# A gMLP kernel whose first column block is written out in one order, with a fourth raw tile and earlier loads

## The chip, the cores and the metric

The kernel runs on one core of one Trainium2 chip, in one launch. The metric is the device time of that core in microseconds. TensorE (PE) multiplies matrices out of SBUF into PSUM banks (8 of 128 x 512 fp32 here), VectorE (DVE) and ScalarE (ACT) work elementwise, GpSimd (POOL) and SyncE (SP) issue DMAs, and ACT issues some too. Each engine takes its instructions in the order in which the program holds them; an instruction that waits holds what stands behind it on its engine.

## The reference

The layer has two halves, each with an adaptive layer norm: a state space convolution (half A), whose code the change leaves alone, and a gated MLP (half B) over 2048 tokens of width 576 with 4608 hidden columns. Half B is what this text is about:

```python
z = _gelu(jnp.einsum("bsd,df->bsf", x, w_in))
z1 = z[..., :Fh]
z2 = _layernorm(z[..., Fh:], axis=-1)
g = jnp.einsum("ts,bsf->btf", w_sp, z2) + b_sp[None, :, None]
return jnp.einsum("bsf,fd->bsd", z1 * g, w_out)
```

`Fh` is 2304, `w_sp` is 2048 x 2048 and mixes tokens, so g needs the whole of z2 before its first column can be made.

## The kernel before, in words

Half A and the making of z2 fill the first 692 us. z2 lies then in memory (`z2_d`), normalized. What follows, `phase_b` (line 1629), takes the output tokens in four **column blocks** q = 0 to 3 of 512. All products are made in fp16 with a high and a low part: a fp32 matrix X becomes hi = fp16(X) and lo = X - hi, and a product takes three matmuls (hi hi, hi lo, lo hi). For w_sp x z2 and for w_in x the input, a scheme of seven products in place of eight is used, so each operand is first turned into seven tiles of sums: this is a **set** (`zset`, 128 x 7 x 2 x 256 fp16).

In one block, nine steps f = 0 to 8 each do the following.
- Two **z1 units**: gelu(x w_in) for 128 columns each. In block 0 this is `z1_unit`: 14 matmuls 128 x 512 with weights `wf` loaded from `win_d`. In blocks 1 to 3 it is `z1_pair` with a set of w_in (`zset` again, 42 matmuls with `n2o`), plus 6 matmuls `ps<-n2r,wr` for the last 64 rows of w_in; those rows (`wr`) are loaded by SP (`wr_load`) and scaled on ACT (`wr_scale`, L1427). PE's results are copied by ACT (L1461), summed by DVE (L1458) and put through gelu on ACT.
- **g_products**: g = w_sp x z2 for 256 columns, four **groups** n = 4f to 4f + 3 of 42 matmuls 128 x 256, `ps<-wsp,zset`, 168 in all, into four PSUM banks. Each group has its own set of z2; the eight tiles `wsp` of w_sp belong to the block.
- **g_unit**, the gate: DVE adds the products with the bias into the single tile `gt` (six instructions, L1525), multiplies with z1 (L1540), ACT writes the high part (L1542), DVE subtracts (L1544), ACT writes the low part (L1546). The next step's products need the banks that L1525 frees.

After the nine steps `out_block` multiplies with w_out (`ps<-wout,z`, 432 matmuls 128 x 288), while DVE and ACT build the next block's `n2o` and `wsp` tiles; each half row of output passes ACT (L1574) and DVE (L1575 to L1577) and a whole row is written by a DMA that ACT issues (L1604).

**Where the sets come from.** In block 0 each set of z2 is built: SP loads 512 KB into a tile `raw` (`z2_load`), DVE forms the sums (L1036, L1037), ACT the high part (L1091), DVE the low part (L1092), which frees the raw tile. Two sets of three are then stored to `set_d` by a DMA that ACT issues; groups with n % 3 == 2 are built again in block 1 and stored there. All others are loaded by POOL (L1489). In block 1 the sets of w_in are built too: four DMAs into a raw tile (`wa_raw`), DVE L1411 to L1414, ACT L795, DVE L801. The raw tiles also take the reads of `w_spT`, from which the next block's `wsp` tiles are made, and other transfers: three tiles in all. A load that has no free tile waits on SP's queue, with every load behind it.

**What sets the order.** The products on PE are pinned in the order of the program (line 129 is the helper that pins, so pinned instructions carry L129). In block 0, `ahead` is called for each group: it asks for the set three further on (`ready`), whose load is issued `AHEAD` = 3 built sets ahead (`more`). The rest on DVE and ACT is placed by a scheduler of the framework, from the instructions that could go next. In `out_block` and its builds DVE, ACT and PE are all pinned (`self.nc = self.last`).

Of the kernel before, what the change touches and what calls it, by code (L numbers as in the profile page):

```python
# [765 lines left out]
class Mlp:  # L766
# [270 lines left out]
        V.tensor_tensor(r[:, 5:7], r[:, 1:4:2], r[:, 4:5].to_broadcast([128, 2, 256]), op=ALU.subtract)  # L1037
# [44 lines left out]
    def z2_load(self, n):  # L1082
        self.nc.sync.dma_start(self.raw(("a", n))[:, :4].rearrange("p k n -> p (k n)"), self.z2_d[n // 4, n % 4].rearrange("p s g c -> p s (g c)"))

    def z2_build(self, n):

        nc = self.nc
        r = self.wss.pop(("a", n))
        o = self.bp.tile([128, 7, 2, 256], F16, name="zset", bufs=3)
        self.z_sums(r)  # L1090
        nc.scalar.activation(o[:, :, 0], r, AF.Copy)  # L1091
        nc.vector.tensor_tensor(o[:, :, 1], r, o[:, :, 0], op=ALU.subtract)  # L1092
        return o


    def x1_load(self, b):
# [320 lines left out]

    def wr_load(self, f):

        wr = self.wrs[f] = self.fp.tile([128, 2, 2, 128], F16, name="wr", bufs=2)  # L1420
        self.nc.sync.dma_start(wr.rearrange("p h k c -> p h (k c)"), self.win_d[f:f + 10:9, :, 8:10].rearrange("h p k c -> p h (k c)"))

    def wr_scale(self, f):

        for h in range(2):
            w, b = self.wrs[f][:, h], R_C + (f + 9 * h) // 4
            self.nc.scalar.activation(w, w, AF.Copy, scale=self.col(b))  # L1427
# [67 lines left out]
    def g_products(self, q, f):  # L1495
# [3 lines left out]
        for i in range(8):  # L1499
            if i % 2 == 0:  # L1500
                n = 4 * f + i // 2
                z = self.zset.pop((q, n))
                if q == self.kept_in(n):
                    self.nc.scalar.dma_start(self.set_d[f, i // 2], z)
                self.ahead(q, n)
# [9 lines left out]
    def g_unit(self, q, f, pg, parts=1):  # L1515
# [11 lines left out]
        def both(pm):  # L1527
            return pm.rearrange("p (o n) -> p o n", o=1).to_broadcast([128, 2, 256])

        add(g1, both(p17[:, 0]), self.bsp[q], neg)  # L1530
        add(g2, both(p6[:, 0]), g1)
        add(g1[:, 0], p54[:, 0], g2[:, 0])
        add(g1, p32, g1)
        add(g2, both(p17[:, 1]), g2, neg)
        add(g2, p54, g2)
# [3 lines left out]
        for c in cs:  # L1539
            V.scalar_tensor_tensor(gt[:, :, c], gt[:, :, c], self.qcol(q, S_P), z1[:, :, c], op0=ALU.mult, op1=ALU.mult)  # L1540
        for c in cs:
            A.activation(p[:, :, 0, c], gt[:, :, c], AF.Copy)  # L1542
        for c in cs:
            V.tensor_tensor(gt[:, :, c], gt[:, :, c], p[:, :, 0, c], op=ALU.subtract)  # L1544
        for c in cs:
            A.activation(p[:, :, 1, c], gt[:, :, c], AF.Copy, scale=2048.0)  # L1546

    def wout_load(self, f):

# [1 line left out]
        self.wss["out", f] = t  # L1551
        self.nc.sync.dma_start(t, self.I["w_out"][128 * f:128 * f + 128])

    def wout_split(self, f):
        self.split(self.wout[:, f, 0], self.wout[:, f, 1], self.wss.pop(("out", f)), self.col(S_O), act=True)

    def out_products(self, pm, q, tt, h, fs):
        T = self.nc.tensor
# [23 lines left out]
    def out_block(self, q):  # L1582
# [5 lines left out]
        for n, (tt, h) in enumerate(halves):  # L1588
# [5 lines left out]
            for k in range(3) if n == 2 else () if n < 2 else (n,):  # L1594
# [8 lines left out]
                elif h == 1:  # L1603
                    A.dma_start(self.out[b], xt)  # L1604

    def phase_b(self):
        self.nc = self.most = Mixed(self.tc, self.tied, "tensor")
        self.last = Mixed(self.tc, self.tied, "vector", "scalar", "tensor")
# [36 lines left out]
        def ahead(q, n):  # L1645
# [1 line left out]
            if isinstance(n, tuple):  # L1647
                return
            f, i = divmod(n, 4)
            if i == 0 and f < 8 and q == 0:  # L1650
                for k in range(units(q, f), units(q, f + 1)):
                    if (q, order[k]) not in self.wfs:
                        self.z1_load(q, order[k])
            if q == 0:
                if ("out", n - 6) in self.wss:
                    self.wout_split(n - 6)
                if 4 <= n < 22:
                    self.wout_load(n - 4)
# [5 lines left out]
        self.ahead = ahead  # L1664
        order = [f + 9 * k for f in range(9) for k in range(2)]

        def units(q, f):

            return max(6, 2 * f + 2)
# [6 lines left out]
        self.wsp_read(self.raw(("b", 7))[:, :4], 0, 7)  # L1676
        more(0, 2)
        self.wsp_build(0, 7)
        for i in range(3, 6):
            self.z1_load(0, order[i])  # L1680
        ready(0, 2)
        for q in range(4):
            done = 0

            def z1(n):
                nonlocal done
                while done < min(n, 18):
                    self.z1_unit(q, order[done])
                    done += 1

            for f in range(9):
# [3 lines left out]
                if q == 0:  # L1695
                    z1(units(q, f))
                else:
                    self.z1_pair(q, f)
                if f == 8 and q < 3:
                    if q == 0:  # L1700
                        self.cfp.close()
                        self.fp = self.pool(self.ctx, "fq", 1, side="right")
                pg = self.g_products(q, f)
                if q and f < 8:
                    self.wr_scale(f + 1)
                if f < 8:
                    self.g_unit(q, f, pg)
                if q == 0:
                    if f == 5:
                        for i in (6, 7):  # L1710
                            self.wsp_load(1, i, None)
                            self.norm_sp(1, i)
                elif q < 3 and f < 6:
# [11 lines left out]
            for i in range(8):  # L1725
                if i == 1:
                    self.scale_gate(q)
                    self.g_unit(q, 8, pg, 2)
                if q < 3:
                    if i == 1:  # L1730
                        self.n2_build(q + 1, 1)
                    self.wsp_build(q + 1, i)
                    block(q + 1, i + 3 if i > 1 else i + 2)
                    if i == 1:
                        self.rows_load(q, 1)
                        block(q + 1, 4)
# [76 lines left out]
```

## Time and profile before

| | us |
|---|---|
| median of 3 runs (1894.89 to 1903.77) | 1895.33 |
| the profiled execution | 1892.11 |
| its span, first to last instruction | 1890.2 |
| PE busy in it | 1702.1 |
| DVE busy | 1268.3 |
| ACT busy | 842.0 |

The mean granted clock of TensorE is 0.961 of full. Times in the views are us from the span's start. A row of a timeline has start, duration, engine, line, operation, output and inputs, the number of instructions run together, and in brackets the idle time before with what ended it. A row of the grouped lines has busy time and mean ns of one, and behind the second bar the idle time before, by releaser. A row of the waits has who waited on what: total, times, longest.

### The profile page before, as it was taken

The numbers are of one execution on the slowest core, as the hardware profiler recorded it, in microseconds if no ns is written. First come the engines' busy times: TensorE is split into PE (matmuls) and PEld (weight loads), VectorE is DVE, ScalarE is ACT, GpSimd is POOL, SyncE is SP. The second block draws the span as 40 slices with busy tenths as digits, with TensorE's granted clock in tenths as the row PEclk, the third lists the DMA queues.
The fourth block names the chain that finished last, engine by engine and source line by source line (L and its number), as shares of the span: only waits on it lengthen the run. The fifth ranks groups of instructions, "written<-read, shape, count | busy, mean of one in ns | idle before, by whom it ended". The sixth has DMA issues, their size and how long they took to land. (4 is left out here: it accounts for less than half of the span.)

```text
span 1890.2 us, 35620 instructions
## 1 busy us (share of the span) xinstructions
PE 1702.1 (90%) x14766; PEld 1257.7 (67%) x14766; DVE 1268.3 (67%) x2352; ACT 842.0 (45%) x1078; POOL 236.8 (13%) x376
## 2 busy tenths in 40 slices
PE   2597999996999998888997968789999999999998
PEld 1254555564555446666676857678888888888887
DVE  8886999848999975866577564657644457544432
ACT  3678999834776663443333323233322213311110
POOL 3211222332222110000000000000011110011100
PEclk9788999998999999998998989999999999999999
DMA  9466556697797885755554656566566564555531
GB/s 251 149 198 204 150 141 166 181 267 239 235 295 250 235 246 191 258 186 189 194 167 155 242 186 219 193 223 208 186 233 221 205 216 154 171 199 207 204 124 39
DMA packets 186914, 377.02 MB, mean 199 GB/s; under 512 B 37536, under 2 KB 107424, under 8 KB 185984
## 3 DMA queue, kind: packets, MB, share of 16 engines
q1 hardware_dynamic: 141840, 157.31, 27.9%
q0 software_dynamic: 36128, 171.57, 27.3%
q10 hardware_dynamic: 8784, 45.86, 6.2%
q8 instruction: 116, 1.90, 0.4%
q14 instruction: 46, 0.38, 0.1%
HBM read 263.94 MB, written 101.31 MB: 193 GB/s over the span
## 5 line engine op out<-in xcount | busy, mean ns | idle before, releaser
L129 PEld LDWEIGHTS <-zset 128*128 128x128 f16 x7182 | 711.5, 100 | 192.1 <-DVE gt L1525 31.3
L129 PE MATMUL ps<-wsp,zset 128*128 128x256 f16 x6048 | 692.6, 278 | 65.9 <-DVE gt L1525 43.3
L129 PE MATMUL pz<-wz,nt 128*128 128x512 f16 (+1 forms) x1120 | 224.7, 361 | 9.2 <-DVE nt L129 5.1
L129 PEld LDWEIGHTS <-nt 128*128 128x128 f16 x1120 | 109.9, 99 | 117.8 <-issue 7.0
L1489 POOL DMA_DIRECT2D zset<-set_d x96 | 50.9, 530 | 980.2 <-PE ps L129 669.7
L129 PE MATMUL ps<-wout,z 128*128 128x288 f16 x1344 | 170.0, 286 | 0.0
L1525 DVE SCALAR_TENSOR_TENSOR gt<-ps,sc,bsp 128x512 f32<-128x512 f32 x32 | 23.9, 748 | 212.4 <-PE ps L129 212.4
L129 PEld LDWEIGHTS <-z 128*128 128x128 f16 x1344 | 131.5, 98 | 33.3 <-issue 0.2
L129 PE MATMUL ps<-n2o,zset 128*128 128x256 f16 x1134 | 132.6, 277 | 20.1 <-DVE zset L801 12.0
L1091 ACT ACTIVATE zset<-raw 128x1792 f16<-128x1792 f32 x48 | 80.8, 1690 | 83.0 <-DVE zset L1092 40.3
L1092 DVE TENSOR_TENSOR zset<-raw,zset 128x1792 f16<-128x1792 f32 x48 | 96.5, 2019 | 27.1 <-ACT zset L1091 27.1
L1525 DVE SCALAR_TENSOR_TENSOR gt<-ps,sc,gt 128x512 f32<-128x512 f32 (+1 forms) x160 | 108.4, 694 | 4.9
L1461 ACT ACTIVATE z<-ps 128x256 f32<-128x256 f32 x42 | 13.8, 379 | 208.6 <-PE ps L129 183.0
L1036 DVE TENSOR_TENSOR raw<-raw 128x256 f32<-128x256 f32 x48 | 20.3, 423 | 102.4 <-DMA raw<-z_d 87.7
L1458 DVE TENSOR_TENSOR z<-ps,z 128x512 f32<-128x512 f32 (+1 forms) x126 | 71.8, 596 | 6.9 <-ACT z L1461 4.3
L129 ACT ACTIVATE wsp<-raw,sc 128x1792 f16<-128x1792 f32 x24 | 42.9, 1787 | 74.4 <-DVE raw L129 74.4
L129 DVE SCALAR_TENSOR_TENSOR wsp<-raw,sc,wsp 128x1792 f16<-128x1792 f32 x24 | 50.0, 2083 | 29.1 <-ACT wsp L129 28.6
L1427 ACT ACTIVATE wr<-wr,sc 128x256 f16<-128x256 f16 x54 | 24.6, 500 | 100.5 <-DMA wr<-win_d 99.0
L129 ACT ACTIVATE z<-pz,sc 128x512 f32<-128x512 f32 (+1 forms) x96 | 52.1, 583 | 13.2 <-PE pz L129 7.5
L395 DVE SCALAR_TENSOR_TENSOR ft<-ft,ps 128x1024 f32<-128x1024 f32 x36 | 43.8, 1216 | 19.8 <-ACT ft L394 19.8
L129 PE MATMUL ps<-n2q,wf 128*128 128x512 f16 x252 | 55.7, 379 | 0.8 <-DMA wf<-win_d 0.8
L1542 ACT ACTIVATE z<-gt 128x1024 f16<-128x1024 f32 x28 | 29.5, 1055 | 60.1 <-DVE gt L1540 60.1
(352 smaller groups left out, 2642.9 us busy)
## 6 DMA issues: line engine op xcount, KB each, us to landing
zset<-set_d POOLq DMA_DIRECT2D x96, 896.0 KB, 4.9
set_d<-zset ACTq DMA_DIRECT2D x36, 896.0 KB, 5.8
raw<-z_d SPq DMA_DIRECT2D x48, 512.0 KB, 5.3
raw<-in_w_spT SPq DMA_DIRECT2D x43, 512.0 KB, 4.3
z_d<-z POOLq DMA_DIRECT2D x32, 576.0 KB, 8.9
zset<-wa_d POOLq DMA_DIRECT2D x18, 896.0 KB, 4.8
u_d<-st1o POOLq DMA_DIRECT2D x16, 576.0 KB, 4.1
u<-u_d SPq DMA_DIRECT2D x36, 256.0 KB, 5.2
```

The source lines that it names most:

```text
L129: return self.tc.keep_in_program_order(f(*a, **k))
L395: V.scalar_tensor_tensor(f, f, MAGIC, pa, op0=ALU.subtract, op1=ALU.subtract)
L1036: V.tensor_tensor(r[:, 4], r[:, 2], r[:, 0], op=ALU.add)
L1091: nc.scalar.activation(o[:, :, 0], r, AF.Copy)
L1092: nc.vector.tensor_tensor(o[:, :, 1], r, o[:, :, 0], op=ALU.subtract)
L1427: self.nc.scalar.activation(w, w, AF.Copy, scale=self.col(b))
L1458: V.tensor_tensor(dst, pm, to, op=ALU.add)
L1461: A.activation(g1[:, k], p17[:, 0], AF.Copy)
L1489: self.nc.gpsimd.dma_start(o, self.set_d[n // 4, n % 4])
L1525: V.scalar_tensor_tensor(dst, pm, by, to, op0=ALU.mult, op1=ALU.add)
L1542: A.activation(p[:, :, 0, c], gt[:, :, c], AF.Copy)
```

## The change

Five things are changed; the computation is the same.

1. **Block 0 in one order.** A new function `first_block` writes block 0 out with DVE, ACT and PE pinned. Within each f it has four parts, one ahead of each group n. A part holds, in varying order: the sums of set n + 4, the high and low part of set n + 2, its store, the load of the next free group; in f = 2 to 7, in the parts 1 to 3, the split of one row block of w_out, with loads two ahead. `g_unit` now returns its five steps, and the part ahead of the first group of f holds the gate sums and the multiplication of f - 1 and the two z1 units, the next part the subtraction and the low part. Four z1 units stand ahead of the first group instead of six.
2. **Four raw tiles** instead of three. The room comes from a smaller DMA scratch (`dynamic_dma_scratch_size=8192`, half of what it was).
3. **wr two pairs ahead.** Three `wr` tiles instead of two; `z1_pair` loads the rows of pair f + 2 behind its matmuls, where it loaded those of f + 1 ahead of them. `wr_scale` is pinned and stands behind the pair's gelu. The scale of pair 0 and the load of pair 1 have moved from ahead of `out_block` to the start of `z1_pair`.
4. **w_spT reads** of the next block go out one tile earlier in `out_block`, and in block 0 the last two of the reads that only serve a norm pass through `gt` in place of raw tiles.

The core of the diff:

```diff
-        t = self.wss[key] = self.bp.tile([128, 7, 256], F32, name="raw", bufs=3)
+        t = self.wss[key] = self.bp.tile([128, 7, 256], F32, name="raw", bufs=4)
...
-        wr = self.wrs[f] = self.fp.tile([128, 2, 2, 128], F16, name="wr", bufs=2)
+        wr = self.wrs[f] = self.fp.tile([128, 2, 2, 128], F16, name="wr", bufs=3)
...
-        if f < 8:
-            self.wr_load(f + 1)
-        z, wr, n2r = self.zset.pop((q, ("w", f))), self.wrs.pop(f), self.n2r
+        if f == 0:
+            self.wr_scale(0)
+            self.wr_load(1)
+        z, wr, n2r = self.zset.pop((q, ("w", f))), self.wrs[f], self.n2r
...
+        if f < 7:
+            self.wr_load(f + 2)
...
-        A.activation(zt, zt, AF.Gelu_apprx_tanh, scale=self.col(INV_C))
+        self.tied.scalar.activation(zt, zt, AF.Gelu_apprx_tanh, scale=self.col(INV_C))
+        if f < 8:
+            self.wr_scale(f + 1)
...
+        def part(f, i):
+
+            n = 4 * f + i
+            if i == 0 and f:
+                gate[:] = self.g_unit(0, f - 1, pgs.pop())
+                gate[0]()
+                hi(n + 2)
+                lo(n + 2)
+                load()
+                gate[1]()
+                if f < 8:
+                    z1()
+                    z1()
+                gate[2]()
+                store(n + 2)
+                sums(n + 4)
+            if i:
+                if i == 1 and f:
+                    gate[3]()
+                if 2 <= f < 8:
+                    k = next(rows)
+                    self.wout_hi(k)
+                    self.wout_lo(k)
+                if f:
+                    sums(n + 4)
+                hi(n + 2)
+                if i == 1 and f:
+                    gate[4]()
+                lo(n + 2)
+                load()
+                store(n + 2)
+                if i == 1 and f in (4, 5):
+                    self.wss[f + 2] = self.bp.tile([128, 2, 512], F32, name="gt", bufs=1).rearrange("p h (k n) -> p (h k) n", n=256)
+                    self.wsp_read(self.wss[f + 2], 1, f + 2)
...
-                    block(q + 1, i + 3 if i > 1 else i + 2)
+                    block(q + 1, i + 4 if i else 2)
...
-                self.wr_scale(0)
...
-    nc = _bacc.Bacc("TRN2", target_bir_lowering=False, num_devices=1)
+    nc = _bacc.Bacc("TRN2", target_bir_lowering=False, num_devices=1, dynamic_dma_scratch_size=8192)
```

How this moves instructions. First DVE in block 0, around one gate (`gt<-ps` are its sums, `gt<-gt,sc,z` the multiplication, `gt<-gt,z` the subtraction; `raw<-raw` are the sums of a set, `zset<-raw,zset` its low part; `wout` rows are w_out's low parts). Before:

```order
L1525 SCALAR_TENSOR_TENSOR gt<-ps,sc,bsp 128x512
L801 SCALAR_TENSOR_TENSOR wout<-gbs,sc,wout 128x576
L1525 SCALAR_TENSOR_TENSOR gt<-ps,sc,gt 128x512
L1092 TENSOR_TENSOR zset<-raw,zset 128x7x256
L1525 SCALAR_TENSOR_TENSOR gt<-ps,sc,gt 128x256
L1036 TENSOR_TENSOR raw<-raw 128x256
L1525 SCALAR_TENSOR_TENSOR gt<-ps,sc,gt 128x512 x2
L1037 TENSOR_TENSOR raw<-raw 128x512
L1525 SCALAR_TENSOR_TENSOR gt<-ps,sc,gt 128x512
L1540 SCALAR_TENSOR_TENSOR gt<-gt,sc,z_7464 128x1024
L1092 TENSOR_TENSOR zset<-raw,zset 128x7x256
L1544 TENSOR_TENSOR gt<-gt,z_7464 128x1024
```

The same place after the change, on DVE again:

```order
L129 SCALAR_TENSOR_TENSOR gt<-ps,sc,bsp 128x512
L129 SCALAR_TENSOR_TENSOR gt<-ps,sc,gt 128x512
L129 SCALAR_TENSOR_TENSOR gt<-ps,sc,gt 128x256
L129 SCALAR_TENSOR_TENSOR gt<-ps,sc,gt 128x512 x3
L129 TENSOR_TENSOR zset<-raw,zset 128x7x256
L129 SCALAR_TENSOR_TENSOR gt<-gt,sc,z_7462 128x1024
L129 TENSOR_TENSOR raw<-raw 128x256
L129 TENSOR_TENSOR raw<-raw 128x512
L129 TENSOR_TENSOR gt<-gt,z_7462 128x1024
L129 SCALAR_TENSOR_TENSOR wout<-xo,sc,wout 128x576
```

The six gate sums now stand together, with nothing of a set or of w_out between them; the set's low part comes behind them.

Second, ACT at the end of block 1's `out_block` and the start of block 2 (`ot<-ps` are output halves, `wsp<-raw` the high parts of the next block's tiles, `z<-ps` the first copies for a z1 pair, `wr` the scales). Before:

```order
L129 ACTIVATE wsp<-raw,sc 128x7x256
L1427 ACTIVATE wr<-wr,sc 128x256 x2
L1574 ACTIVATE ot<-ps 128x288
L1427 ACTIVATE wr<-wr,sc 128x256 x2
L129 ACTIVATE wsp<-raw,sc 128x7x256
L1604 DMA out<-xo 128x576
L1574 ACTIVATE ot<-ps 128x288
L129 ACTIVATE wsp<-raw,sc 128x7x256
L1574 ACTIVATE ot<-ps 128x288
L1604 DMA out<-gt 128x576
L1461 ACTIVATE z_13566<-ps 128x256 x2
```

And ACT there after the change:

```order
L129 ACTIVATE wsp<-raw,sc 128x7x256
L1637 DMA out<-xo 128x576
L1607 ACTIVATE ot<-ps 128x288
L129 ACTIVATE wsp<-raw,sc 128x7x256
L1607 ACTIVATE ot<-ps 128x288
L1637 DMA out<-gt 128x576
L129 ACTIVATE wr<-wr,sc 128x256 x2
L1472 ACTIVATE z_13568<-ps 128x256 x2
L129 ACTIVATE z_13568<-z_13568,sc 128x1024
L129 ACTIVATE wr<-wr,sc 128x256 x2
```

The scale of pair 0 has moved from among the wsp tiles to behind the last output row's DMA.

More of the change, by code (lines that the diff above doesn't have):

```diff
@@ L1604, in out_block, with first_block, load, z1 @@
                     A.dma_start(self.out[b], xt)
+    def first_block(self, order, block):
+        self.nc = self.last
+        A, zset = self.nc.scalar, self.zset
+        groups, units, rows = iter(range(36)), iter(order), iter(range(18))
+        wf = iter(order[3:])
+        def load(n=1):
+            for _, k in zip(range(n), groups):
+                self.z2_load(k)
+        def z1():
+            self.z1_unit(0, next(units))
+            for k in wf:
+                self.z1_load(0, k)
+                break
+        def sums(n):
+            if n < 36:
+                self.z2_sums(n)
+        def hi(n):
+            if n < 36:
+                zset[0, n] = self.z2_hi(n)
+        def lo(n):
+            if n < 36:
+                self.z2_lo(n, zset[0, n])
+        def store(n):
+            if n < 36 and self.kept_in(n) == 0:
+                A.dma_start(self.set_d[n // 4, n % 4], zset[0, n])
+        def part(f, i):
[31 more added lines that the diff above has]
+                    self.wsp_read(self.wss[f + 2], 1, f + 2)
+                if not f:
+                    sums(n + 3)
+                    if i == 3:
+                        sums(n + 4)
+        self.part = part
+        gate, pgs = [], []
+        self.wsp_read(self.raw(("b", 7))[:, :4], 0, 7)
+        load(3)
+        z1()
+        r, o, by = self.wss.pop(("b", 7)), self.wsp_tile(0, 7), self.qcol(0, S_S)
+        self.w_sums(r)
+        self.hi(o[:, :, 0], r, by, act=True)
+        sums(0)
+        hi(0)
+        sums(1)
+        sums(2)
+        self.lo(o[:, :, 1], r, by, o[:, :, 0])
+        z1()
+        lo(0)
+        hi(1)
+        lo(1)
+        z1()
+        store(0)
+        hi(2)
+        lo(2)
+        load(3)
+        z1()
+        store(1)
+        store(2)
+        load()
+        sums(3)
+        for f in range(9):
+            part(f, 0)
+            if f == 1:
+                self.wout_load(0)
+                self.wout_load(1)
+            if f == 8:
+                self.scales_sp(1, self.bank())
+                self.scales_gate(1)
+                self.cfp.close()
+                self.fp = self.pool(self.ctx, "fq", 1, side="right")
+                self.n2_load(1, 0)
+                block(1, 1)
+                self.rows_load(0, 0)
+            pgs.append(self.g_products(0, f))
+            if f == 4 or f == 5:
+                self.norm_sp(1, f + 2)
+            if f == 6:
+                self.sums_sp(1)
+            if f == 7:
+                self.gate_load(0)
+        self.nc = self.most
+        return pgs.pop()
@@ L1649, in ahead @@
             f, i = divmod(n, 4)
[L1650 to L1658, printed above, removed]
             if f == 8 and q < 3 and i == 1:
@@ L1675, in phase_b @@
         bp.tile([128, 288], F32, name="ot", bufs=2)
[L1676 to L1681, printed above, removed]
-        for q in range(4):
[L1683 to L1691, printed above, removed]
+        pg = self.first_block(order, block)
+        for q in range(4):
+            for f in range(9) if q else ():
                 if f == 8 and q < 3:
```

99 lines of the change are left out of this document (51 added, 48 removed).

## The prediction

> **What bounds the kernel now.** I began with the windows of 100 us (start and end, length, busy time and instructions of PE, PEld, DVE, ACT and POOL, granted clock, DMA share, GB/s), to see in which stage TensorE is not the bound.
>
> ```profile
> 700.00:800.00 100.00, 82.10 (x622) 62.23 (x621) 66.99 (x73) 40.33 (x35) 0.67 (x1) 0.93 0.62 220
> 800.00:900.00 100.00, 85.96 (x640) 64.88 (x638) 66.29 (x76) 42.07 (x41) 0.00 (x0) 0.91 0.53 194
> 900.00:1000.00 100.00, 93.44 (x745) 72.96 (x743) 69.26 (x103) 32.65 (x30) 1.13 (x2) 0.98 0.52 174
> ```
>
> In column block 0, which lies here, PE idles 7 to 18 us of each 100 and the granted clock falls with it, while no other engine is over 70%. The chain of waits says where that ends:
>
> ```profile
> 1205.88 7.25 DMA raw<-in_w_in
> 1256.61 628.68 PE ps L129 x5555
> ```
>
> After 1256.6 us PE alone sets the end; before it the chain goes through loads into raw tiles. So a us won in blocks 0 and 1 is a us at the end, and a us lost in blocks 2 and 3 is one too. Next, PE's timeline, for what the stages would take without waits:
>
> ```profile
> 692.18 15.27 PE L129 MATMUL ps<-n2q,wf 128*128 128x512 f16 x70
> 846.98 6.21 PE L129 MATMUL ps<-n2q,wf 128*128 128x512 f16 x28
> 853.02 1.15 PE L129 MATMUL ps<-wsp,zset 128*128 128x256 f16 x9
> 966.78 5.31 PE L129 MATMUL ps<-wout,z 128*128 128x288 f16 x42
> 1018.45 1.63 PE L129 MATMUL ps<-wout,z1b 128*128 128x288 f16 x12
> 1037.12 8.13 PE L129 MATMUL ps<-wsp,zset 128*128 128x256 f16 x73
> 1351.10 4.75 PE L129 MATMUL ps<-n2o,zset 128*128 128x256 f16 x42
> 1355.68 1.03 PE L129 MATMUL ps<-n2r,wr 128*128 128x256 f16 x6
> 1356.55 18.50 PE L129 MATMUL ps<-wsp,zset 128*128 128x256 f16 x168
> 1374.89 4.75 PE L129 MATMUL ps<-n2o,zset 128*128 128x256 f16 x42
> ```
>
> From start to start, 168 g matmuls take 18.34 us (4.585 a group of 42), a pair of z1 units in block 0 6.04, in later blocks 5.45. Block 0 runs from 692.18 to 966.78, 274.6 us; nine g and 18 z1 units need 9 x 18.34 + 9 x 6.04 = 219.4. It loses 55: in the three windows 38 us are idle (the shortfall of busy from 100), and some 17 go to a lower clock (7 + 9 + 2%). The way from block 0's last output matmul (about 1020.1) to g of block 1 at 1037.1 takes 17 where 5.45 are needed: 11.6 lost. For block 1's body the lines grouped from 1037 to 1260 us give the work:
>
> ```profile
> L129 PE MATMUL ps<-wsp,zset 128*128 128x256 f16 x1214 | 144.3, 283 | 28.2 <-DVE gt L1525 26.4 <-DVE zset L1092 1.7
> L129 PE MATMUL ps<-n2o,zset 128*128 128x256 f16 x294 | 36.0, 282 | 10.2 <-DVE zset L801 10.2
> L1036 DVE TENSOR_TENSOR raw<-raw 128x256 f32<-128x256 f32 x10 | 4.2, 423 | 37.2 <-DMA raw<-z_d 22.6 <-issue 7.4 <-ACT zset L795 7.2
> L1411 DVE TENSOR_TENSOR raw<-raw 128x256 f32<-128x256 f32 x7 | 3.0, 425 | 37.5 <-DMA raw<-in_w_in 37.5
> L129 ACT ACTIVATE raw<-raw 128x1024 f32<-128x1024 f32 x8 | 8.3, 1043 | 1.1 <-DMA raw<-in_w_spT 1.1
> L1427 ACT ACTIVATE wr<-wr,sc 128x256 f16<-128x256 f16 x16 | 7.3, 500 | 71.8 <-DMA wr<-win_d 71.8
> ```
>
> 1214 x 18.34/168 + 7 x 5.45 = 171 of 223 us: 52 lost.
>
> **Block 0's one order.** What DVE and ACT waited for from 680 to 1030 us, and what SyncE's queue did from 690 to 1020:
>
> ```profile
> DVE raw L1036 <- DMA raw<-z_d: 65.1, 26, 7.4
> PE ps L129 <- DVE zset L1092: 18.6, 9, 5.7
> PE ps L129 <- DVE gt L1525: 16.9, 9, 4.8
> SPq L129 <- DVE zset L1092: 176.9, 29, 11.8
> ```
>
> DVE waits for z2 groups, whose loads wait in SyncE's queue for a raw tile; the tile is freed by the low half L1092 of an older group. PE then waits for a group (18.6) or for its banks behind late gate sums (16.9). The change gives a fourth tile, asks for each group earlier, and takes sums and gate steps in a written order. Whether DVE and ACT keep the pace follows from the durations:
>
> ```profile
> L1092 DVE TENSOR_TENSOR zset<-raw,zset 128x1792 f16<-128x1792 f32 x36 | 72.3, 2018 | 13.2 <-ACT zset L1091 13.2
> L1525 DVE SCALAR_TENSOR_TENSOR gt<-ps,sc,gt 128x512 f32<-128x512 f32 (+1 forms) x40 | 27.0, 691 | 0.4
> L1037 DVE TENSOR_TENSOR raw<-raw 128x512 f32<-128x512 f32 x36 | 24.7, 687 | 0.7
> L1540 DVE SCALAR_TENSOR_TENSOR gt<-gt,sc,z 128x1024 f32<-128x1024 f32 x7 | 8.9, 1278 | 0.1
> L1544 DVE TENSOR_TENSOR gt<-gt,z 128x1024 f32<-128x1024 f32 x7 | 8.5, 1219 | 1.3 <-ACT z L1542 1.1
> L801 DVE SCALAR_TENSOR_TENSOR wout<-gbs,sc,wout 128x576 f16<-128x576 f32 x9 | 7.3, 810 | 1.1 <-ACT wout L795 1.1
> L795 ACT ACTIVATE wout<-gbs,sc 128x576 f16<-128x576 f32 x9 | 6.9, 772 | 17.9 <-DMA gbs<-in_w_out 11.7 <-DVE gt L1525 6.2
> ```
>
> One f costs DVE four groups of 0.42 + 0.69 + 2.02 = 12.5, a gate of six adds at about 0.7 plus 1.28 and 1.22 = 6.6, three w_out low parts 2.4: 21.6 us, against PE's 24.4. But the written order couples the engines. In the last two parts of an f, ACT issues a store of the set only once L1092 is done (0.34, as the DMA issue rows of the last part below), then scales w_out (0.77); DVE takes w_out's low part (0.81), sums (1.11), the next low part (2.02): about 5.1 a group where PE takes 4.6. The first part holds 4.1 of gate sums, a low part, 1.3 and 1.1, 8.5 us, under the z1 pair and a group, 10.6; the second 5.2. Together some 24 of 24.4 us: it fits, with nothing over for a load that lands late. Two groups stand ready ahead of PE, so one late load is absorbed, a rate is not. Two reads of w_spT now go through the single gate tile in f = 4 and 5: issued in the second part, when the gate is done with it, they have the 14 us of three groups to land and be squared on ACT (1.04, in the ACT raw row above) before the next gate's sums, so I cost them at nothing; landing later than that, they would hold those sums. The loads themselves move the same bytes in less time: from the three windows' 196 GB/s on average to about 230, a little above the first window's 220.
>
> At the start four z1 units instead of six are written: 692.18 + 12.1 = 704.3, and g begins near 706 (1.7 lost, set 0's low half being last). The gate of the first f is late, I put 2.3 us of wait and about 3 of slow clock; for each of the six f with w_out 1 us of lateness. That is 13 left of 55, a gain of **42**. The bounds: all 55 but the start, 50, and 25 where every f pays 3 us and a slow stretch.
>
> **Block 1.** The 25 uses of a raw tile there (10, 7 and 8 above) in 223 us make one in 8.9 us, so with a fourth tile a load can go out one use, some 8.9 us, sooner. One of the waits on DVE, PE's beside it, and the longest on ACT:
>
> ```profile
> 1089.22 0.43 DVE L1411 TENSOR_TENSOR raw<-raw 128x256 f32<-128x256 f32 x1 [9.19 <-DMA raw<-in_w_in]
> 1094.43 0.80 PE L129 MATMUL ps<-wsp,zset 128*128 128x256 f16 x3 [8.93 <-DVE gt L1525]
> 1125.37 0.91 ACT L1427 ACTIVATE wr<-wr,sc 128x256 f16<-128x256 f16 x2 [14.44 <-DMA wr<-win_d]
> ```
>
> DVE idled from 1080.0, where its last instruction freed the tile that the w_in load was queued for, to the landing 9.2 us later; the gate sums that PE needs stand behind L1411 in DVE's order. 8.9 us sooner ends that wait; wr asked two pairs ahead ends the 14.4 us on ACT, whose next work is the copy L1461 for the pair. What remains is order: w_in's sums still stand ahead of the gate's, and the sets are asked for no earlier. From the 37.5 + 22.6 us of DVE's waits and their slow clock I leave 20 of the 52: a gain of **32**; bounds 12 (only the wr part and two or three of the waits go) and 45. The wr load, now behind the pair's matmuls on SyncE's queue, has some 48 us to land in a third buffer; the w_spT reads that go out one tile earlier in the output block take the fourth raw tile, where PE has 53 us of output matmuls (966.8 to 1020.1) as cover: both at nothing. At the entry to block 1 the first w set comes one wsp tile sooner, but wr(0) is now scaled behind the last output row: **+1** (-2 to +3).
>
> **Blocks 2 and 3.** Here the change costs. The scale of wr(0), pinned now, has moved behind the last output's DMA issue on ACT:
>
> ```profile
> 1358.12 0.34 ACTq L1604 DMA_DIRECT2D out<-gt  x1
> 1624.69 0.34 ACTq L1604 DMA_DIRECT2D out<-gt  x1
> 1622.88 1.03 PE L129 MATMUL ps<-n2r,wr 128*128 128x256 f16 x6
> 890.60 18.18 PE L129 MATMUL ps<-wsp,zset 128*128 128x256 f16 x153 [2.28 <-DVE gt L1525]
> 890.00:893.50 3.50, 2.90 (x15) 0.53 0.76 263
> ```
>
> PE wants wr at 1355.68; ACT can have it at 1358.46 + 2 x 0.5 = 1359.5: 3.8 us, and all g matmuls queue behind. In block 3, 1626.0 against 1622.9: 3.1. A wait of 2.28 us was followed by a clock of 0.53 for 3.5 us, 1.7 lost; both waits are longer, so twice 1.7 more. Together **-10** (-3 if the output row ends sooner, -14 with a double stretch).
>
> [...]
>
> **The sum.** 42 + 32 + 1 - 10 = 65. The profiled execution took 1892.1 us (span 1890.2 and 1.9 around it), so 1827; the median is 3.2 above it: **1830 us**. Half a per cent, 9.5 us, is about what a measurement can tell from no change. The pool's halved DMA scratch I cost at nothing: POOL is busy under 1% in block 0's windows, and no row shows its queue full; if it did stall, the sets of blocks 2 and 3 would show it.
>
> **The rivals.**
> - *Block 1 keeps its waits* (the w_in sums still ahead of the gate's, the loads late again because everything asks sooner): for it, that the number of sets asked ahead is unchanged; against, the tile that was missing at 1080. Gain 42 + 5 + 1 - 10 = 38: 1857. Chance 0.2.
> - *Block 1 comes near PE's bound*, and the wr stalls cost 5: 45 + 40 + 2 - 5 = 82: 1813. Chance 0.2.
> - *Slower: head of the line in block 0.* In a written order a late group stops DVE, and with it gate, w_out and the next groups; today's scheduler lets others pass. If loads took the 14.4 us that ACT waited for wr, instead of the 7 to 9 of the raw loads quoted, then with about 5 us of lead two groups in each f would be 9 us late, 18 an f less the 2 x 1.2 that the ready groups win back, some 15 x 8 = 120 lost where 55 are lost now; less 23 gained elsewhere that is 42 above now, 1937. It decides from landings of about 11 us. Against: the 26 waits for groups today average 2.5. Chance 0.05.
> - *It does not do what it says* (the raw tiles still end late, the order only trades one wait for another): within 10 us of now. Chance 0.05.
>
> The forecast case has 0.5. The range leaves out the last two and the far ends of the first two: 1804 (gains of 48 and 45, entry 2, wr -4) to 1864 (30, 12, -1, -10). Faster by over 0.5% 0.90 (the first three cases), within it 0.05, slower 0.05.
>
> **What would show it.** Block 0 ending near 925 instead of 966.8; no "DVE raw <- DMA raw<-z_d" over 3 us; the w_in waits of block 1 under 3 us each and the wr wait on ACT gone; PE waits of 3 to 4 us ahead of the first n2r matmuls of blocks 2 and 3, and none from there on. Wrong if block 0 gains under 25, if the PE waits for gate sums in block 1 stay at 6 to 9 us, or if PE idles inside blocks 2 and 3.

## The result and the profile after

| | before | after |
|---|---|---|
| median, us | 1895.11 (1893.41 to 1903.77, 4 runs) | 1845.76 (1843.18 to 1848.96, 4 runs) |
| ratio | | 0.9718, interval 0.9694 to 0.9741 |
| span of the profiled execution | 1890.2 | 1841.4 |
| mean granted clock | 0.961 | 0.973 |

The change saves 49 us; 65 were forecast. The windows of both stages, with the columns of the windows shown in the prediction, first of the kernel before (block 0 from its first z1 matmul to its first output matmul, block 1 from its first g matmul to its first output matmul), then of the changed one:

```profile
692.18:966.78 274.60, 236.12 (x1769) 177.28 (x1766) 183.34 (x239) 107.72 (x97) 2.60 (x3) 0.94 0.58 203
1037.12:1298.20 261.08, 222.70 (x1901) 189.26 (x1899) 152.55 (x223) 84.14 (x97) 12.69 (x24) 0.93 0.64 220
```

```profile
695.15:928.76 233.61, 222.11 (x1769) 173.46 (x1767) 189.98 (x243) 110.79 (x99) 2.60 (x3) 0.98 0.71 244
998.14:1244.02 245.88, 217.57 (x1899) 187.12 (x1898) 151.01 (x220) 83.10 (x95) 12.71 (x24) 0.96 0.66 229
```

Block 0 is 41.0 us shorter, block 1 only 15.2. PE's timeline of block 0 after the change shows that what is still lost lies at its start:

```profile
695.15 9.23 PE L129 MATMUL ps<-n2q,wf 128*128 128x512 f16 x42
705.54 3.19 PE L129 MATMUL ps<-n2q,wf 128*128 128x512 f16 x14 [1.16 <-DMA wf<-win_d]
717.22 0.61 PE L129 MATMUL ps<-wsp,zset 128*128 128x256 f16 x2 [8.48 <-ACT zset L129]
719.69 20.07 PE L129 MATMUL ps<-wsp,zset 128*128 128x256 f16 x166 [1.86 <-DVE zset L129]
739.60 6.21 PE L129 MATMUL ps<-n2q,wf 128*128 128x512 f16 x28
745.64 18.50 PE L129 MATMUL ps<-wsp,zset 128*128 128x256 f16 x168
...
910.42 18.50 PE L129 MATMUL ps<-wsp,zset 128*128 128x256 f16 x168
928.76 5.31 PE L129 MATMUL ps<-wout,z 128*128 128x288 f16 x42
```

From 739.6 on there is not one wait: g takes 18.34 us from start to start and the pair 6.04 in every f. All of the 14.2 us that block 0 still loses (233.6 against the 219.4 needed) lie ahead of that. Block 1 after the change (PE's timeline) still waits for gate sums, and the starts of blocks 1 and 2 wait for wr:

```profile
996.46 1.89 PE L129 MATMUL ps<-n2r,wr 128*128 128x256 f16 x6 [3.85 <-ACT wr L129]
...
1077.28 0.80 PE L129 MATMUL ps<-wsp,zset 128*128 128x256 f16 x3 [5.06 <-DVE gt L1541]
...
1142.96 18.64 PE L129 MATMUL ps<-wsp,zset 128*128 128x256 f16 x153 [8.11 <-DVE gt L1541]
...
1304.34 1.22 PE L129 MATMUL ps<-n2r,wr 128*128 128x256 f16 x6 [2.65 <-ACT wr L129]
```

At block 3's start the wait is 1.95. What ACT, DVE and PE waited for in block 1 (waits from 998 to 1244 us: total, times, longest):

```profile
ACT z L1564 <- DVE gt L1560: 50.1, 7, 13.0
DVE raw L1036 <- DMA raw<-z_d: 42.9, 8, 8.9
PE ps L129 <- DVE gt L1541: 26.7, 12, 8.1
DVE raw L1419 <- DMA raw<-in_w_in: 16.8, 3, 5.8
```

The w_in waits went from 37.5 to 16.8 us, those for z_d rose from 22.6 to 42.9, and the 71.8 us of ACT for wr are gone (its row has 0.0 now). In sum DVE waits for loads as long as before (60.1 and 59.7), and so does PE for gate sums: 26.4 us in 10 waits before, 26.7 in 12 now. What PE no longer waits for is the sets of w_in, 10.2 us before and 0.3 now, and its clock is a little higher (0.93 before, 0.96 now).

All runs below are read by these stages, since block 0 starts anywhere from 691.8 to 701.8 us in profiles of kernels that are the same up to there (708.3 in c_raw5, for a likely reason given last); what makes that spread was not looked into. Lengths in us; "entry" is from the first output matmul to the next block's first g matmul, where 52.9 + 5.45 = 58.4 are needed; block 1 needs 9 x 18.34 + 8 x 5.45 = 208.7.

| kernel | median | block 0 | entry 1 | block 1 | entry 2 | entry 3 |
|---|---|---|---|---|---|---|
| before | 1895.1 | 274.6 | 70.3 | 261.1 | 58.4 | 58.4 |
| after | 1845.8 | 233.6 | 69.4 | 245.9 | 61.4 | 60.7 |
| b_raw4 | 1883.3 | 266.1 | 64.0 | 259.9 | 58.4 | 58.4 |
| b_raw4_wr | 1885.3 | 266.1 | 73.2 | 249.0 | 61.4 | 60.4 |
| a_place | 1833.8 | 224.6 | 68.5 | 245.6 | 61.4 | 60.5 |
| a_wr0 | 1836.7 | 232.0 | 66.8 | 247.9 | 58.4 | 58.4 |
| c_base | 1825.6 | 224.3 | 66.2 | 248.1 | 58.4 | 58.4 |
| c_ahead4 | 1822.1 | 224.5 | 65.1 | 242.3 | 58.4 | 58.4 |
| c_raw5 | 1869.6 | 239.6 | 58.4 | 266.8 | 58.4 | 58.4 |
| c_nonorm | 1836.9 | 227.1 | 66.7 | 253.8 | 58.4 | 58.4 |
| c_kept0 | 1808.9 | 231.1 | 66.5 | 221.6 | 58.4 | 58.4 |
| d_pinv | 1821.1 | 225.6 | 65.7 | 232.0 | 58.4 | 58.4 |
| e_kept0_pinv | 1792.5 | 228.6 | 66.5 | 209.5 | 58.4 | 58.4 |
| e_kept0_pinva | 1821.0 | 231.5 | 63.8 | 239.3 | 58.4 | 58.4 |

Each median was taken beside runs of the kernel before, whose median was 1895 to 1898.5 each time. Blocks 2 and 3 take 208.7 to 209.2 in all, but for 214.9 in block 2 of d_pinv's profile. Each length is from one profiled execution. Kernels whose code agrees in a stage show how far it varies: block 1 is 245.6 to 248.1 in the changed kernel, a_place, a_wr0 and c_base; block 0 is 224.3 to 227.1 in a_place, c_base, c_ahead4, c_nonorm and d_pinv. So in these two blocks a difference of under 3 us says nothing.

### The profile page after: what moved, and what is told of

It is laid out like the page before. It is cut to its first block, busy times and chain, and to the rows that moved or that the text cites. A ratio compares the mean times of both kernels' runs of the same rounds, so it can differ in the third digit from the quotient of the medians.

```text
span 1841.4 us, 35610 instructions
## 1 busy us (share of the span) xinstructions
PE 1684.4 (91%) x14766; PEld 1251.9 (68%) x14766; DVE 1270.2 (69%) x2352; ACT 841.8 (46%) x1078; POOL 237.2 (13%) x376
## 4 chain that ended last, share of the span: by engine, by line
PE 44%; DVE 18%; DMA 8%; issue 6%; ACT 4%; SPq 1%; POOL 1%; ACTq 0%; DVEq 0%; POOLq 0%
PE ps L129 41%; DMA raw<-z_d 3%; DVE raw L129 2%; DVE bsz L129 2%; ACT wsp L129 2%; DVE n L129 1%; DVE wsp L129 1%; DVE gt L129 1%; DMA raw<-in_w_in 1%; DVE gt L1541 1%; SPq L129 1%; DVE rq L129 1%; DVE wso L129 1%; DVE zset L1096 1%; DVE zset L801 1%
## 5 line engine op out<-in xcount | busy, mean ns | idle before, releaser
L129 PE MATMUL ps<-wsp,zset 128*128 128x256 f16 x6048 | 676.2, 274 | 38.4 <-DVE gt L1541 26.7
L1541 DVE SCALAR_TENSOR_TENSOR gt<-ps,sc,bsp 128x512 f32<-128x512 f32 x24 | 18.0, 749 | 221.7 <-PE ps L129 221.7
L129 DVE TENSOR_TENSOR raw<-raw 128x256 f32<-128x256 f32 (+2 forms) x177 | 94.7, 540 | 9.5 <-DMA raw<-z_d 4.4
L1541 DVE SCALAR_TENSOR_TENSOR gt<-ps,sc,gt 128x512 f32<-128x512 f32 (+1 forms) x120 | 81.4, 695 | 4.5
L129 ACT ACTIVATE zset<-raw 128x1792 f16<-128x1792 f32 x36 | 60.9, 1691 | 43.7 <-PE ps L129 25.4
L129 DVE TENSOR_TENSOR zset<-raw,zset 128x1792 f16<-128x1792 f32 x36 | 72.6, 2019 | 10.9 <-ACT zset L129 10.9
L1469 DVE TENSOR_TENSOR z<-ps,z 128x512 f32<-128x512 f32 (+1 forms) x126 | 71.8, 596 | 7.1 <-ACT z L1472 3.8
L129 ACT ACTIVATE z<-pz,sc 128x512 f32<-128x512 f32 (+1 forms) x96 | 51.7, 584 | 16.1 <-DMA z_d<-z 10.3
L129 ACT ACTIVATE z<-z,nm,r 128x1152 f32<-128x1152 f32 x24 | 31.5, 1342 | 53.2 <-DVE nm L129 29.9
L129 PE MATMUL ps<-wout,z1b 128*128 128x288 f16 x384 | 52.3, 286 | 0.0
```

The lines of the kernel that those rows point to most:

```text
L129: return self.tc.keep_in_program_order(f(*a, **k))
L1541: V.scalar_tensor_tensor(dst, pm, by, to, op0=ALU.mult, op1=ALU.add)
```

## The experiments

**The parts alone.** b_raw4 is the kernel before with the tile and its room, nothing else (the list of the change has four points, not five; the smaller scratch stands under its second):

```diff
-        t = self.wss[key] = self.bp.tile([128, 7, 256], F32, name="raw", bufs=3)
+        t = self.wss[key] = self.bp.tile([128, 7, 256], F32, name="raw", bufs=4)
...
-    nc = _bacc.Bacc("TRN2", target_bir_lowering=False, num_devices=1)
+    nc = _bacc.Bacc("TRN2", target_bir_lowering=False, num_devices=1, dynamic_dma_scratch_size=8192)
```

> The kernel before with four raw tiles and the smaller DMA scratch, nothing else. Theory 1 (the missing tile is the main cause in both blocks): blocks 0 and 1 lose 25 us less between them, about 1870. Theory 2 (block 0's gain is the written order with its earlier asking, block 1's is the tile): about 10 us less in block 0, 10 in block 1, about 1878. In either case, if the late start of block 0 in the changed kernel comes from where the fourth tile puts the last wsp tile in memory, ACT's high part of that tile waits for a z_d store here too, some 5 us or more.

It ran at 0.9926 (0.9905 to 0.9947). The tile gives block 0 8.5 us and the entry 6.3; block 1's 1.2 is within the spread. Theory 2 had block 0 about right and block 1 wrong. Over all of block 1 (1024.5 to 1284.4 us) the tile did end most of PE's wait for w_in's sets, 1.1 us against 10.2, but 9.3 for sets of z2 (1.7 before) and 3.3 for copies of the output came in its place, and 21.1 for gate sums stayed. ACT does wait for a z_d store at block 0's start here too (ACT's timeline). What waits is a copy into a z1 tile, with the wsp part behind it; the kernel before has no such wait (its ACT makes that copy at 701.49 and the wsp part at 702.08). So this comes with the tile and not with the order:

```profile
702.48 1.24 ACT L1482 ACTIVATE z<-ps,sc 128x512 f32<-128x512 f32 x2
711.62 0.69 ACT L1482 ACTIVATE z<-ps,sc 128x512 f32<-128x512 f32 x1 [7.90 <-DMA z_d<-z]
712.20 1.78 ACT L795 ACTIVATE wsp<-raw,sc 128x1792 f16<-128x1792 f32 x1
```

b_raw4_wr adds the change's edits of `wr_load`, `wr_scale`, `z1_pair` (with the gelu pinned) and `block`, so it is the whole change without block 0's order.

> As b_raw4, with the wr part and the earlier w_spT reads of the change as well: all of the change but block 0's written order. If wr on ACT was a part of block 1's wait, block 1 gains 5 or more over b_raw4, and the starts of blocks 1 to 3 pay some 8 us for the moved scale: within 5 us of b_raw4. If wr was covered by the other waits, block 1 is as in b_raw4 and the time is 5 to 8 us above it. The difference to the changed kernel is what the written order of block 0 is worth: 30 or more is expected.

0.9941 (0.9920 to 0.9962). Block 1 gains 10.9 over b_raw4; the three starts are 9.2, 3.0 and 2.0 us longer, where PE waits for the moved scale (6.83, 2.64 and 1.68 us): together nothing won. The first of these waits (PE's timeline):

```profile
1033.69 1.89 PE L129 MATMUL ps<-n2r,wr 128*128 128x256 f16 x6 [6.83 <-ACT wr L129]
```

What b_raw4's ACT waited for fits the 10.9 (waits from 990 to 1230 us; over all of its block 1 it is 57.0 us):

```profile
ACT wr L1427 <- DMA wr<-win_d: 59.6, 9, 14.1
```

With the load two pairs ahead this wait is gone, and PE's waits for sets and output copies in block 1 fall from 13.7 to 2.3 us, while those for gate sums do not fall (21.1, then 24.7). That the wr load alone did it is not shown: the pinned gelu and the earlier w_spT reads came with it.

The rest, 266.1 to 233.6 in block 0, is the written order, with its earlier asking and the two reads through `gt`: 32.5 us.

**Block 0's start.** After the change ACT waited for a store, and the first set's high part stood behind (ACT's timeline):

```profile
705.12 0.67 ACT L129 ACTIVATE z<-ps,sc 128x512 f32<-128x512 f32 x1
713.79 1.79 ACT L129 ACTIVATE wsp<-raw,sc 128x1792 f16<-128x1792 f32 x1 [8.01 <-DMA z_d<-z]
715.48 1.68 ACT L129 ACTIVATE zset<-raw 128x1792 f16<-128x1792 f32 x1
```

The wsp tile has nothing to do with z_d, so I took the wait for one on the tile's memory. a_place gives it its place ahead of the raw tiles:

```diff
         bp.tile([128, 288], F32, name="ot", bufs=2)
+        bp.tile([128, 7, 2, 256], F16, name="wsp")
         pg = self.first_block(order, block)
```

> The changed kernel with one line more, which gives the wsp tile of the last index its place in memory ahead of the raw tiles. Theory (place): block 0's first g group waits 8.5 us because that tile lies over the z tiles that the last z_d stores still read; placed elsewhere the group starts near 711 instead of 717 and the time falls by 6 to 9 us. Rival (the stores themselves set it, since the sets need z2's last rows): no change beyond 2 us.

0.9672 (0.9654 to 0.9690); block 0 is 9.0 us shorter, and ACT's rows there are

```profile
705.25 1.78 ACT L129 ACTIVATE wsp<-raw,sc 128x1792 f16<-128x1792 f32 x1
706.93 1.68 ACT L129 ACTIVATE zset<-raw 128x1792 f16<-128x1792 f32 x1
708.51 0.67 ACT L129 ACTIVATE z<-ps,sc 128x512 f32<-128x512 f32 x1
709.08 1.69 ACT L129 ACTIVATE zset<-raw 128x1792 f16<-128x1792 f32 x1
712.95 0.69 ACT L129 ACTIVATE z<-ps,sc 128x512 f32<-128x512 f32 x1 [2.18 <-DMA z_d<-z]
```

What is left is a later, shorter wait, on a z1 tile. Moving the wsp tile's place ended its wait, as the place theory has it; by the rival, that the stores set the start in any case, nothing would have changed. That the fourth tile had pushed the wsp tile onto memory which the last stores of z2 still read follows from this run and b_raw4 together; no address was read, and the tiles behind it moved too.

**The wr scale.** a_wr0 scales wr(0) ahead of the output block again, unpinned, and keeps the rest:

```diff
     def wr_scale(self, f):
+        nc = self.tied if f else self.most
...
-        if f == 0:
-            self.wr_scale(0)
-            self.wr_load(1)
+        if f == 0:
+            self.wr_load(1)
...
                 self.bias_load(q + 1)
+                self.wr_scale(0)
```

> The changed kernel with the scale of wr(0) back ahead of the output block, the rest of the wr part kept. The trace shows PE waiting 3.85, 2.65 and 1.95 us for it at the starts of blocks 1, 2 and 3: if these waits are its price, 7 to 9 us less. If something else is late right behind, under 3 us.

0.9679 (0.9646 to 0.9712); entries 2 and 3 are back at 58.4, entry 1 gains 2.6: 7.9 in all, the price of the three waits. Its runs spread from 1827.65 to 1842.9 us, so the stages are the surer reading. c_base has this edit and a_place's.

> The changed kernel with the two small edits that the last six runs share (the wsp tile placed first, the scale of wr(0) moved back) and nothing else. Block 0 near 225, block 1 from its first g group 245 to 248, no wait at the starts of blocks 2 and 3; 9 + 8 us below the changed kernel, about 1829. If block 1 were under 240 here, the gains read for the pinned order and the stored sets would be too large by as much.

0.9618 (0.9600 to 0.9636): 1825.6 us where about 1829 was expected, with the stages as expected. The next runs are c_base with one thing changed in each.

**What holds block 1.** Four theories: the loads are asked for too late (ask), they lack tiles, there are too many bytes, or DVE's order puts sums that wait for a load ahead of urgent work (order).

```diff
# c_ahead4
-        AHEAD = 3
+        AHEAD = 4
# c_raw5
-        t = self.wss[key] = self.bp.tile([128, 7, 256], F32, name="raw", bufs=4)
+        t = self.wss[key] = self.bp.tile([128, 7, 256], F32, name="raw", bufs=5)
# with dynamic_dma_scratch_size=2048
# c_nonorm
-        self.nsp = self.sums(32 + 8 * q, 8)
+        self.nsp = self.sums(32 + 8 * (1 if q == 2 else q), 8)
...
-                if q < 3 and f < 6:
+                if 1 < q < 3 and f < 6:
# c_kept0
-        return 1 if n % 3 == 2 else 0
+        return 0
```

> The changed kernel with the wsp tile placed first and the scale of wr(0) moved back, and the sets of blocks 1 asked for four ahead instead of three. All four kernels here have the first two edits, so blocks 0, 2 and 3 should be as in those runs, and what is read is the length of block 1 from its first g group to its output, 245 to 248 us so far where PE needs 208.7. Theory ask (loads are issued too late by the program): block 1 falls to 230 or less. Theory tile (four tiles are all taken, an earlier ask only queues): 245 within 4, since the load still goes out when a tile comes free. Theory order (sums of a set stand ahead of the gate's sums on DVE): 245 within 4 unless the scheduler's order changes with it.

0.9599 (0.9562 to 0.9636), block 1 242.3: 5.8 of the 39 that c_base's 248.1 loses, far from the 230 of the ask theory and within what tile or order allow. The intervals of the two kernels overlap, so even the 5.8 is not sure; PE's waits changed in kind (13.6 us for gate sums against 22.2, 9.5 for w_in's sets against 3.1).

> As the first of this call but asked three ahead, with a fifth raw tile (room from a DMA scratch of 2048 bytes). Theory tile: one use more, some 8 us earlier for each load that waits: block 1 at 230 or less. Theory ask: the loads are issued by the program no earlier, 243 or more. If the smaller scratch stalls the sets that GpSimd loads, blocks 2 and 3 are over 209.

0.9841 (0.9817 to 0.9864): worse than c_base. Block 1 takes 266.8, with 35.5 us of waits for gate sums; nothing here speaks for the tile theory. It is no clean test, since the small scratch seems to have done harm elsewhere (last section), and why block 1 became longer than in c_base was not settled; its DVE order is another one. The entry to block 1, though, is without loss there.

> The eight reads of w_spT that block 1 makes for the norm of block 2 are left out, with their squares on ACT; block 2's scale is taken from block 1's norm. Eight uses of a raw tile of about 27 and 4 MB of loads fewer in block 1. Theory tile or bytes: block 1 at 232 or less. Theory order or ask: 241 or more, since z_d and w_in loads are still asked for as late as now.

0.9673 (0.9645 to 0.9701), block 1 253.8, 5.7 longer than c_base with 4 MB and eight tile uses fewer. That fewer bytes and tile uses did not help speaks against both as the main cause; that less work takes longer points to the order, which the scheduler makes anew for each kernel. For the same reason it is not proof: the order changed with the bytes.

> All 36 sets of z2 are stored in block 0, so block 1 builds only w_in's sets and GpSimd loads the rest: 12 z_d loads, their sums and low parts, and 12 raw uses leave block 1, and 12 more stores of 0.9 MB come into block 0. If the late z_d loads ahead of the gate's sums are what holds block 1 (DVE waits 43 us on them): block 1 at 220 or less; block 0 grows by 0 to 10 us from the stores. If the bytes moved are what holds it (they rise by 4.6 MB net in block 1): no less than 243.

0.9537 (0.9501 to 0.9573). Without z_d loads block 1 falls to 221.6, by 26.5; block 0, with 12 more stores, is 6.8 longer (228.6 to 231.5 in the three kernels that have them, against the 224.3 to 227.1 above). (The expectation's count of bytes forgot the 12 stores that leave block 1: it moves some 6 MB fewer, not 4.6 more. But 4 MB fewer won nothing in c_nonorm.) So it is the z_d sets, by their place or by themselves. How their place hurts is in the rows of the changed kernel, DVE's first:

```profile
1074.54 0.42 DVE L1036 TENSOR_TENSOR raw<-raw 128x256 f32<-128x256 f32 x1 [8.90 <-DMA raw<-z_d]
1074.99 0.69 DVE L1037 TENSOR_TENSOR raw<-raw 128x512 f32<-128x512 f32 x1
1075.61 0.74 DVE L1541 SCALAR_TENSOR_TENSOR gt<-ps,sc,bsp 128x512 f32<-128x512 f32 x1
```

and ACT's, the high parts of the z_d sets:

```profile
1072.96 1.70 ACT L1091 ACTIVATE zset<-raw 128x1792 f16<-128x1792 f32 x1 [1.56 <-DMA wa_d<-zset]
...
1098.33 1.70 ACT L1091 ACTIVATE zset<-raw 128x1792 f16<-128x1792 f32 x1 [7.38 <-PE ps L129]
```

The set summed at 1074.5 can't be the one of 1072.96, whose high part began before; its own high part is made at 1098.3, 23 us later. DVE stood 8.9 us for data that nobody needed yet, and PE 5.06 us for the gate sums behind. d_pinv keeps tiles, loads and bytes, and pins DVE in block 1 to the order of the program:

```diff
         for q in range(4):
+            if q == 1:
+                self.nc = Mixed(self.tc, self.tied, "vector", "tensor")
             for f in range(9) if q else ():
```

> The changed kernel with the wsp tile placed first and the scale of wr(0) moved back, and in block 1 DVE pinned to the order in which the program is written: a set is summed only when it is to be made, two sets ahead of PE, and the gate's sums come behind the sets of their own step. Tiles, loads and bytes are as they were. Theory order (the scheduler puts sums of sets that PE needs much later ahead of the gate's sums, and DVE then waits for loads that are not urgent): block 1 falls from 245 to 222 or less. Theory ask, tile or bytes: 240 or more, since the loads go out no earlier.

0.9604 (0.9570 to 0.9639), block 1 232.0: 16 us less than c_base, but not the 222 or less of the order theory, nor the 240 or more of the others. In its waits (990 to 1230 us) gate sums cost PE 0.4 us, where c_base's PE waits 22.2 for them, and small waits for sets have come, 16.7 us in all:

```profile
PE ps L129 <- DVE zset L129: 9.3, 8, 1.7
PE ps L129 <- DMA zset<-set_d: 4.0, 3, 1.8
PE ps L129 <- ACT zset L1091: 3.4, 3, 2.2
PE ps L129 <- DVE gt L129: 0.4, 1, 0.4
```

So the order was a cause, about 16 of 39 us; with it mended, z_d's sets cost most of the other 23, as the next run shows. e_kept0_pinv has both edits.

> The same with all sets stored in block 0, as in c_kept0, whose block 1 took 221.6. Theory order: the late z_d loads hurt only by their place in DVE's order, so with the order pinned there is little left that storing all sets could win: block 1 within 5 us of d_pinv's, block 0 some 6 us longer as in c_kept0, and the time no better than d_pinv's by more than 3 us. If z_d's loads cost by themselves (bytes, tiles): block 1 under 214 and 8 us or more below d_pinv's.

0.9447 (0.9418 to 0.9476), **1792.5 us**: the fastest version, better than both kernels. Block 1 takes 209.5 of 208.7. The expectation by the order alone (no gain over d_pinv) missed: z_d's sets cost by themselves, on top of their place. Whether by their loads, their tiles or their work on DVE and ACT was not separated. The shares depend on which is mended first: order first, 16.1 and then 22.5 for the sets; sets first (c_kept0), 26.5 and then 12.1 for the order. e_kept0_pinva pins ACT as well.

> As e_kept0_pinv (1792.5), with ACT pinned in block 1 too. Block 1 is within a us of PE's bound already, so the theory that order on DVE was the cause expects no change beyond 2 us; if ACT's order matters now that DVE's is fixed, block 1 gets longer or the entry shorter by more than 2.

0.9590 (0.9562 to 0.9618): block 1 29.8 us longer. ACT's rows, first with ACT free (e_kept0_pinv), then pinned, of the high part of a w_in set and the issue of that set's store:

```profile
1047.96 1.79 ACT L795 ACTIVATE zset<-raw,sc 128x1792 f16<-128x1792 f32 x1 [1.70 <-PE ps L129]
1051.90 0.40 ACTq L1445 DMA_DIRECT2D wa_d<-zset  x1
```

```profile
1058.26 1.77 ACT L129 ACTIVATE zset<-raw,sc 128x1792 f16<-128x1792 f32 x1
1072.52 1.06 ACT L129 ACTIVATE z<-gt 128x1024 f16<-128x1024 f32 x1 [12.48 <-DVE gt L129]
1074.87 1.06 ACT L129 ACTIVATE z<-gt 128x1024 f16<-128x1024 f32 x1 [1.29 <-DVE gt L129]
1074.93 0.33 ACTq L129 DMA_DIRECT2D wa_d<-zset  x1
```

In the program's order the store stands behind the gate and goes out 16.7 us after the start of the high part instead of 3.9. PE then waits 21.7 us for sets that GpSimd loads (0 before). That the late store keeps its tile from the next set is my reading: a load of GpSimd starts at 1079.09, 4.2 us behind the store, but the profile puts that load's wait down to DVE. Pinning wins only where the written order is the better one.

## Why the prediction was right or wrong

- **Block 0, 42 forecast, 41.0 measured.** The size is right, the steps are not. I left 1 us of lateness in each of six f and about 5 us for the first gate: neither is there. I put the start at 1.7 us: it loses 1.2 + 8.5 + 1.9 us of waits and 2.7 more of the 14.2, most of it at a lower clock (0.50 from 717.22 to 719.69 us, 0.52 from there to 723.50). The step that failed there is "g begins near 706": it looked at the work and not at where a new tile lies. The two errors cancel, so the match of 42 and 41 is luck.
- **Entry 1, +1 forecast, +0.9 measured.** Both sides came as said: PE waits 2.48 us for the first w set where it waited 8.07, and 3.85 for wr, with a clock of 0.58 from 996.0 to 998.5 us.
- **Block 1, 32 forecast, 15.2 measured: the term that was mis-sized.** The step "8.9 us sooner ends that wait" failed: PE's wait for gate sums is 26.7 us where it was 26.4, and the fourth tile alone gives 1.2 us. The other half, the edits around wr, which I took for the lesser part, gives 10.9 of the 15.2. That is near my lower bound of 12, whose condition (the wr part and a few waits) is about what happened. The rest that I named, sums ahead of the gate's and sets asked for no earlier, was larger than the 20 I left: 37 us (39 in c_base), of which the runs give 16 to the order and, not surely, 5.8 to asking earlier. My rival "block 1 keeps its waits" had that mechanism and put the gain at 5; the measurement lies between the two.
- **Blocks 2 and 3, -10 forecast, -5.3 measured.** The mechanism is right, shown by a_wr0. The waits were 2.65 and 1.95 instead of 3.8 and 3.1: PE goes on after the first of the two scales, not both (in block 2 they begin at 1303.78, PE at 1304.34), and neither wait slowed the clock (1.00 in the 3.7 us behind each).
- **The slower rival.** Block 0 has a single wait of DVE for z_d left, 4.4 us; the head of the line that I priced for block 0 is what block 1 suffers from, where the scheduler and not the hand put a waiting sum first.
- **The signs that I named.** Block 0 ended at 928.8, near the 925 named, ACT's wr wait is gone, and blocks 2 and 3 lose nothing after their starts (208.8 and 208.7). But the w_in waits of block 1 are up to 5.8 us, not under 3, and of PE's waits there for gate sums one is still 8.1 and one 5.1 us: the sign for block 1's account being wrong has come in part.
- The sum: 41.0 + 0.9 + 15.2 - 5.3, less 3.0 for block 0's later start, is 48.8, the difference of the spans.

## What to carry to other kernels

A load that comes late is only as bad as what stands behind its first user on that engine's queue (in the changed kernel DVE stood 8.9 us for a set whose high part came 23 us later, and PE 5.06 us for the gate sums behind it): look at when the data is needed next, and write the order so that urgent sums stand ahead of a wait. Another buffer can change where later tiles lie: here the wsp tile's high part waited 8.0 us, by my reading for a store that still read the memory it came to lie on, and block 0 was 9.0 us shorter with the tile's place given first. And undo the parts one by one: here the part meant as a detail (the edits around wr) and the one meant as the cure (a fourth tile) had changed places in block 1, and 8 us of the former's gain were given back at the block starts.

## What the runs showed of the hardware

**Short waits and the clock.** Windows of the changed kernel behind a wait of 2.65 us, behind three of 2.75, 0.80 and 1.76 us within 7.3 us, and behind one of 8.11 us (the clock is the last figure but two):

```profile
1304.30:1308.00 3.70, 3.65 (x30) 2.86 (x31) 2.60 (x5) 0.93 (x3) 0.00 (x0) 1.00 0.91 317
1203.00:1207.00 4.00, 3.62 (x34) 3.25 (x35) 3.97 (x7) 1.06 (x1) 0.20 (x1) 1.00 0.57 233
1142.90:1146.50 3.60, 3.54 (x17) 2.55 (x18) 3.50 (x6) 1.06 (x1) 0.00 (x0) 0.50 0.00 0
```

Behind the 2.65 us the clock was 1.00, behind the three waits too, behind the 8.11 us 0.50, and behind one of 2.28 us in the kernel before it was 0.53; the latter came less than a us of matmuls after another wait of 0.61 (PE's timeline before):

```profile
887.49 0.83 PE L129 MATMUL ps<-wsp,zset 128*128 128x256 f16 x6 [0.61 <-DVE gt L1525]
```

Why the clock was lower behind 2.28 us than behind 2.65, no run shows. One row was too little to price the clock by.

**GpSimd's DMA scratch.** With 2048 bytes (c_raw5), GpSimd's stores of z_d no longer went out in pairs (its timeline, then the same in the changed kernel with 8192):

```profile
713.62 1.01 POOL L129 DMA_DIRECT2D z_d<-z  x1 [7.94 <-issue]
719.35 1.01 POOL L129 DMA_DIRECT2D z_d<-z  x1 [4.72 <-issue]
```

```profile
704.42 1.01 POOL L129 DMA_DIRECT2D z_d<-z  x1 [10.40 <-ACT z L129]
705.62 1.01 POOL L129 DMA_DIRECT2D z_d<-z  x1 [0.19 <-issue]
```

The second store follows after 5.7 us instead of 1.2, and block 0 starts at 708.3. The scratch is the likely cause, but c_raw5 has a fifth tile too, and no run has the small scratch alone. I had expected the harm in blocks 2 and 3, which show none (208.8). With 8192 bytes the two stores stand 1.2 us apart as in the kernel before (698.42 and 699.66 there), so no cost of the smaller scratch shows there, as forecast.
